# Windowed attention with a spatial gating block: spread of n, bias tables, weight conversion, size of the score groups, order

## The chip, the cores and the metric

The kernel runs on one core of a Trainium2 chip. What counts is the device time of one launch in microseconds (us). Before the change three runs took 471.61, 471.88 and 472.74 us, a median of 471.88 us. PE is TensorE with its matrix multiplications and PEld its weight loads; DVE is VectorE, ACT is ScalarE, POOL is GpSimd, and SP is SyncE, whose queue issues all DMAs here.

## What is computed

Attention over 4 batches, 8 heads and 768 tokens of 64 numbers; each token sees the first `n_global` (8) tokens and the last `n_local` (96), with a bias that falls with distance. Its output goes through a block that mixes the tokens of half of its features with a 768 x 768 matrix and multiplies the result with the other half.

```python
scores = scale * np.matmul(q, k.transpose(0, 1, 3, 2))
rel = pos[:, None] - pos[None, :]
is_global = pos[None, :] < int(n_global)
is_local = (rel >= 0) & (rel < int(n_local))
keep = is_global | is_local
dist = np.where(is_global & ~is_local, float(n_local), np.abs(rel))
scores = np.where(keep, scores + -slopes[:, None, None] * dist, -1e9)
a = softmax(scores)                       # along the keys
x = (a @ v)                               # heads side by side: 768 x 512 a batch
h = np.maximum(x @ w_in, 0.0)
u, v = h[..., :512], h[..., 512:]
v_n = (v - mean(v)) / np.sqrt(var(v) + 1e-06)
v_s = np.einsum('ts,bsd->btd', w_spatial, v_n) + b_spatial[None, :, None]
return (u * v_s) @ w_out
```

`w_in` and `w_out` come in as 64-bit floats, the rest as 32-bit floats, `n_global` and `n_local` as 64-bit integers.

## The kernel before

**Blocks.** The 768 tokens of a batch are 6 blocks of 128, so there are 24 blocks, numbered n over all batches. A block has scores against itself and, but for the first block of a batch, the block before it; the few global keys are copied into the ring of keys (`kring`).

**Steps of a block.** `scores(n)` (L1167) multiplies q and k for the 8 heads. Heads go in pairs, one on each 64-row half of PE; a pair is a matmul for either half, written side by side as one recorded operation (`halves64`, L122). VectorE takes the scores of a head from a PSUM bank, adds the bias table and finds the smallest entry (here called an eviction; `pr<-bank,bias` in the trace, followed by the reading of its result into `mn`), ScalarE takes the exponential (`pr<-pr,mn`), GpSimd or VectorE divides by the sum (`pr<-pr,rc`). `values(n)` (L1238) transposes the eight results on PE (`bank<-ident,pr`), copies them (`pth`), multiplies by v (`ops<-pth,vring`), and splits the result into a high and a low half (`xth`, `xtl`). The later matmuls use such halves, three products for one.

**The first six blocks** use whole 32-bit floats for q and k, one product for a pair. From block 6 on it is three products of halves. `size` (L1193) is the number of pairs in a group of scores: 4 in the first block of a batch, whose scores are 128 wide, else `SG`, which is 2. From block 6 on, a group of 2 is 12 matmuls and one of 4 is 24. A group is never broken by other work of PE, and holds a PSUM bank for every two pairs and half of rows where scores are 256 wide: two banks for a group of 2, four for a group of 4.

**Gating block.** `mlp_v`, `mlp_u`, `mlp_s` and `mlp_o` (L1277 to L1354; V, U, G and O in the schedule) are the four matrix products of the second part. They read `w_in`, `w_t` (the spatial matrix) and `w_out`, each as a high and a low half.

**Front.** Before that the kernel must load and build: the two numbers n (`nraw`, `nf`, `nwide`), the bias tables from them (`setup_bias`, L990: `bias0` for the first block of a batch, `bias` for the others, eight heads each), and the halves of the weights. `split_weights` (L1055) turns a tile of 128 x 512 64-bit floats into 32-bit halves: 8 tiles of `w_in`, 4 of `w_out`. It takes the sign apart, scales and clamps the upper word, shifts it into place and puts the sign on (the shift-and-or), masks the exponent out (the mask), multiplies the lower word by it (the product), and adds up. The tiles are `u`, `gh`, `gl` (as loaded), `raw`, `rawh` and `ev` in SBUF, and a PSUM bank.

**What sets the order.** All of this is first recorded, not issued. `plan` (L383) then sets every operation's place on its engine. It goes through time with a cost for every operation (`cost`, L243), a list of ranks (`RANKS`, L574: the lowest ready rank goes first) and pins (`PINS`, L827: the engine for an operation that could run on several), and it hands out six PSUM banks; two more hold `ops`. So a change in the number of operations needs new lists. Where the plan has a gap of more than 0.9 us on PE between 3.8 and 150 us, `keep_warm` (L544) fills it with transposes of the identity, `bank<-ident` in the trace. Nearly all instructions have the lines L47 or L49 in the trace, where they are issued.

Of the kernel before, what the change touches and what calls it, by code (L numbers as in the profile page):

```python
# [242 lines left out]
def cost(op):  # L243
# [6 lines left out]
    if op.eng == "tensor":  # L250
        if op.call == "transpose":
            return 109, 0, False
        if op.call == "halves64":
            n = elements(op.args[0]["rhs"])
            if op.args[0]["rhs"].dtype == F32:
                return 50 + len(op.args) * max(109, n * (.844 if list(op.args[0]["rhs"].ap)[0][1] < P else .422)), 0, False
            return len(op.args) // 2 * max(107, n * .461), 0, False
        n = elements(op.kw["rhs"])
        if op.kw["rhs"].dtype == F32:
            return max(234, 4 * n * .422), 0, False  # L260
        return {128: 111, 256: 120, 384: 177, 512: 232}[n], 0, False
    if op.eng == "sync":
        if n * parts <= 512:
            return 450, 600, False
        run = n // list(out.ap)[-1][1] * parts
        return (450 if run <= P and parts == P else 600 if run <= 256 else 1250), 120 + n * 4 * parts * .00243, False
# [27 lines left out]
    return (190 if parts < P else 74) + 1.04 * n + (0 if one else 60), 0, not one  # L294
# [249 lines left out]
def keep_warm(order, make):  # L544
# [996 lines left out]
```

## Time and profile before

| | us |
|---|---|
| median of 3 runs | 471.88 |
| the profiled execution | 472.18 |
| its span, first to last instruction | 470.4 |
| PE busy | 457.1 |
| VectorE busy | 313.3 |
| ScalarE busy | 202.6 |
| GpSimd busy | 180.6 |

The profiled execution's own time is 1.8 us longer than its span, and 0.3 us above the median. Busy time is a union of an engine's instructions; identity transposes count as busy on PE. In the trace a bank, a ring or a work tile has its name without its number. In a timeline, equal neighbours are drawn together with a count; matmuls overlap, so the pace of a run is the time from its start to the next start. An `issue` in the chain of waits is time in which an engine waited for nothing that the profile shows.

### The profile page before, as it was taken

How to read it: one execution, taken by the hardware profiler on the slowest of the kernel's cores; microseconds unless marked ns; L12 is line 12 of the kernel's file. 1: busy time of each engine (PE TensorE's matmuls, PEld its weight loads, DVE VectorE, ACT ScalarE, POOL GpSimd, SP SyncE). 2: the span in 40 equal slices, each digit the busy share in tenths (PEclk: the TensorE clock that was granted, in tenths of full speed). 3: DMA queues.
4: the chain of work that ended last, by engine and by line, in shares of the span. 5: the costliest groups of instructions: out<-in, count | busy, mean ns of one | idle time of the engine just before them, and what ended most of it. 6: DMA issues, size and time to landing. Idle time of an engine off the chain costs nothing.

```text
span 470.4 us, 9937 instructions
## 1 busy us (share of the span) xinstructions
PE 457.1 (97%) x3734; PEld 404.8 (86%) x3734; DVE 313.3 (67%) x947; ACT 202.6 (43%) x582; POOL 180.6 (38%) x285
## 2 busy tenths in 40 slices
PE   8888899999999999999999999999999999999996
PEld 8666679899888889889998889989998888989995
DVE  5999899973587678673338598985404688842343
ACT  2988665310364566652004675652113187320001
POOL 3788754451146656420115354351003163420021
PEclk9999899999999999999999999999999999999999
DMA  6947322410222323220012034220101211000012
GB/s 233 340 156 240 108 74 90 139 49 24 67 55 75 123 75 80 84 76 1 1 45 88 33 118 140 52 91 1 29 0 47 72 48 51 7 1 1 22 46 75
DMA packets 17816, 35.98 MB, mean 76 GB/s; under 512 B 2400, under 2 KB 2656, under 8 KB 17760
## 3 DMA queue, kind: packets, MB, share of 16 engines
q1 hardware_dynamic: 17760, 35.27, 22.9%
q8 instruction: 31, 0.51, 0.5%
q14 instruction: 25, 0.20, 0.1%
HBM read 28.97 MB, written 6.29 MB: 75 GB/s over the span
## 4 chain that ended last, share of the span: by engine, by line
PE 85%; DVE 9%; ACT 2%; POOL 1%; issue 1%; DMA 1%; SPq 0%; DVEq 0%; ACTq 0%; POOLq 0%
PE bank L49 71%; PE ops L47 7%; PE bank L47 7%; DVE bank L49 2%; DVE ev L49 2%; DVE pr L49 2%; POOL pr L49 1%; DMA nraw<-in_n_local_dram 1%; ACT pr L49 1%; DVE bias L49 1%; DVE w_in_l L49 1%; DVE rawh L49 0%; DVE raw L49 0%; DVE xtl L49 0%; ACT w_in_h L49 0%
## 5 line engine op out<-in xcount | busy, mean ns | idle before, releaser
L49 ACT ACTIVATE pr<-pr,mn 128x256 f32<-128x256 f32 (+1 forms) x192 | 92.3, 482 | 37.8 <-DVE mn L49 33.5
L49 DVE CUSTOM_DVE_ANT_0 pr<-bank,bias 128x256 f32<-128x256 f32 (+1 forms) x192 | 69.5, 395 | 27.7 <-PE bank L47 15.2
L49 POOL TENSOR_SCALAR pr<-pr,rc 128x256 f32<-128x256 f32 (+1 forms) x118 | 60.5, 525 | 45.9 <-DVE rc L49 34.2
L49 PE MATMUL bank<-ident,pr 128*128 128x128 f32 x352 | 59.1, 279 | 4.2 <-POOL pr L49 3.5
L49 ACT ACTIVATE ev<-bank 128x512 f32<-128x512 f32 (+1 forms) x37 | 21.5, 581 | 79.6 <-PE bank L49 38.7
L49 ACT ACTIVATE pth<-bank 128x512 f32<-128x512 f32 (+1 forms) x62 | 33.5, 552 | 50.3 <-PE bank L49 38.9
L49 PEld LDWEIGHTS bank<-ident,pr 128*128 128x128 f32 x352 | 41.5, 141 | 15.4 <-POOL pr L49 7.4
L49 DVE TENSOR_TENSOR ev<-bank,b_bc 128x512 f32<-128x512 f32 x24 | 16.4, 688 | 49.1 <-PE bank L49 46.1
L47 PE MATMUL bank<-kring,q 64*128 64x256 f32 (+1 forms) x528 | 46.4, 310 | 0.5 <-POOL kring L49 0.3
L49 PE MATMUL bank<-w_t_l,vnh 128*128 128x256 f32 x288 | 45.6, 283 | 0.0
L49 PE MATMUL bank<-w_t_h,vnh 128*128 128x256 f32 x288 | 44.7, 284 | 0.0
L49 PE MATMUL bank<-w_t_h,vnl 128*128 128x256 f32 x288 | 44.7, 282 | 0.0
L47 PEld LDWEIGHTS bank<-kring,q 64*128 64x128 f32 x528 | 36.0, 188 | 9.3 <-issue 4.2
L47 PE MATMUL ops<-pth,vring 128*64 128x128 f32 x704 | 43.7, 276 | 0.0
L47 PEld LDWEIGHTS ops<-pth,vring 128*64 128x64 f32 x704 | 37.9, 137 | 4.9 <-issue 3.4
L49 PEld LDWEIGHTS bank<-w_t_l,vnh 128*128 128x128 f32 x288 | 39.3, 189 | 1.0
L49 PEld LDWEIGHTS bank<-w_t_h,vnh 128*128 128x128 f32 x288 | 38.8, 189 | 0.9
L49 PEld LDWEIGHTS bank<-w_t_h,vnl 128*128 128x128 f32 x288 | 38.8, 189 | 0.9 <-issue 0.2
L49 ACT ACTIVATION_READ_ACCUMULATOR pr<-pr,mn 128x1 f32 x192 | 36.3, 189 | 0.0
L49 PE MATMUL bank<-xth,w_in_h 128*128 128x256 f32 x192 | 34.5, 289 | 0.5 <-DVE mn L49 0.5
L49 PE MATMUL bank<-xth,w_in_l 128*128 128x256 f32 x192 | 33.9, 287 | 0.0
L49 PE MATMUL bank<-xtl,w_in_h 128*128 128x256 f32 x192 | 33.6, 287 | 0.0
(127 smaller groups left out, 859.8 us busy)
## 6 DMA issues: line engine op xcount, KB each, us to landing
vring<-in_v_dram SPq DMA_DIRECT2D x24, 256.0 KB, 2.8
out_dram<-ev SPq DMA_DIRECT2D x23, 256.0 KB, 2.0
u<-in_moe_w_in_dram SPq DMA_DIRECT2D x8, 512.0 KB, 5.5
raw<-in_q_dram SPq DMA_DIRECT2D x9, 256.0 KB, 2.8
rawh<-in_q_dram SPq DMA_DIRECT2D x9, 256.0 KB, 2.6
raw<-in_k_dram SPq DMA_DIRECT2D x9, 256.0 KB, 2.7
rawh<-in_k_dram SPq DMA_DIRECT2D x9, 256.0 KB, 2.7
kring<-in_k_dram SPq DMA_DIRECT2D x6, 256.0 KB, 5.2
```

The lines of the kernel that those rows point to most:

```text
L47: self.real.matmul(**{n: placed(x) for n, x in kw.items()})
L49: getattr(self.real, self.call)(*[placed(x) for x in self.args], **{n: placed(x) for n, x in self.kw.items()})
```

## The change

Five things change.

- The numbers n are loaded to one partition instead of 128, turned into floats there, and spread by a matmul against a row of ones; VectorE copies the result from PSUM.
- The bias tables are built from maxima and minima with a large number instead of products with masks, in fewer steps. The scaling of `bias0` may run on ScalarE or GpSimd too.
- In `split_weights` the clamp comes before the scaling, the scaled tile goes to a PSUM bank, and the later steps go back and forth so that the shift-and-or, the product and both additions read at least one operand from PSUM. The mask reads SBUF and writes PSUM. The signed zero and the clamp are each done by VectorE or GpSimd.
- From block 6 on, a group of scores has four pairs.
- Some costs of the planner, all ranks and all pins are new, so the order is new on every engine.

```diff
 CFG = {
-    "WS": 6, "SG": 2, "WG": 4, "kept": "p", ...
+    "WS": 6, "conv": "pp", "SG": 4, "SG0": 2, "WG": 4, "kept": "p", ...
@@ cost
-            return len(op.args) // 2 * max(107, n * .461), 0, False
+            return 87 + len(op.args) // 2 * max(107, n * .461), 0, False
...
+    if op.call == "tensor_scalar" and not one and isinstance(op.kw.get("scalar1"), bass.AP):
+        return 130 + .54 * n, 0, True
...
-    return (190 if parts < P else 74) + 1.04 * n + (0 if one else 60), 0, not one
+    return (190 if parts < P else 74) + 1.04 * n + (0 if one else 60), 0, not (one and ("accum_out" in op.kw or any(in_psum(x) for x in op.reads) or len(op.reads) < 2))
@@ RANKS
-    -660.98, -553.57, -397.00, -559.33, ...
...
@@ attn_then_spatial_gating_kernel
-    nraw = const.tile([P, 4], I32, name="nraw")
-    nc.sync.dma_start(out=nraw[:, 0:2], in_=n_global.bitcast(I32).partition_broadcast(P))
-    nc.sync.dma_start(out=nraw[:, 2:4], in_=n_local.bitcast(I32).partition_broadcast(P))
-    nf = const.tile([P, 4], F32, name="nf")
+    nraw = const.tile([1, 4], I32, name="nraw")
+    nc.sync.dma_start(out=nraw[:, 0:2], in_=n_global.bitcast(I32).partition_broadcast(1))
+    nc.sync.dma_start(out=nraw[:, 2:4], in_=n_local.bitcast(I32).partition_broadcast(1))
+    row = const.tile([1, P], F32, name="row")
+    nc.vector.memset(row, 1.0)
+    nf = const.tile([1, 4], F32, name="nf")
...
+    spread = ps_m.tile([P, 2], F32, name="spread", tag="cv")
+    nc.tensor.matmul(spread, lhsT=row, rhs=none, start=True, stop=True)
+    nc.vector.tensor_copy(out=nwide, in_=spread)
@@ setup_bias
-        ts(out=g, in0=col, scalar1=ng, scalar2=None, op0=ALU.is_lt)
-        ts(out=far, in0=g, scalar1=-BIG, scalar2=BIG, op0=ALU.mult, op1=ALU.add)
-        ts(out=far, in0=far, scalar1=nl, scalar2=None, op0=ALU.add)
-        ts(out=loc, in0=rel, scalar1=nl, scalar2=None, op0=ALU.is_lt)
-        stt(out=loc, in0=rel, scalar=0.0, in1=loc, op0=ALU.is_ge, op1=ALU.mult)
-        tt(out=d_b, in0=rel, in1=loc, op=ALU.mult)
-        ts(out=t, in0=loc, scalar1=-1.0, scalar2=1.0, op0=ALU.mult, op1=ALU.add)
-        tt(out=d_0, in0=far, in1=t, op=ALU.mult)
-        tt(out=d_0, in0=d_0, in1=d_b, op=ALU.add)
+        ts(out=relp, in0=rel, scalar1=0.0, scalar2=BIG, op0=ALU.is_lt, op1=ALU.mult)
+        tt(out=relp, in0=relp, in1=rel, op=ALU.max)
+        ts(out=relb, in0=rel, scalar1=float(P), scalar2=None, op0=ALU.add)
+        ts(out=out_b, in0=relp, scalar1=nl, scalar2=BIG, op0=ALU.is_ge, op1=ALU.mult)
+        ts(out=g, in0=col, scalar1=ng, scalar2=BIG, op0=ALU.is_ge, op1=ALU.mult)
+        tt(out=d_b, in0=relp, in1=out_b, op=ALU.max)
+        stt(out=d_0, in0=g, scalar=nl, in1=d_b, op0=ALU.add, op1=ALU.min)
         for h in range(H):
-            ts(out=bias0[:, h], in0=d_0, scalar1=-slopes[h] / scale, scalar2=None, op0=ALU.mult)
+            scaled(None, bias0[:, h], d_0, -slopes[h] / scale)
         def more():
-            stt(out=d_b, in0=t, scalar=BIG, in1=d_b, op0=ALU.mult, op1=ALU.add)
-            ts(out=rel, in0=rel, scalar1=float(P), scalar2=None, op0=ALU.add)
-            ts(out=loc, in0=rel, scalar1=nl, scalar2=None, op0=ALU.is_lt)
-            ts(out=t, in0=loc, scalar1=-BIG, scalar2=BIG, op0=ALU.mult, op1=ALU.add)
-            tt(out=d_a, in0=rel, in1=loc, op=ALU.mult)
-            tt(out=d_a, in0=d_a, in1=t, op=ALU.add)
-            nc.vector.tensor_copy(out=d_a[:, 0:NGMAX], in_=far[:, 0:NGMAX])
+            ts(out=out_a, in0=relb, scalar1=nl, scalar2=BIG, op0=ALU.is_ge, op1=ALU.mult)
+            tt(out=d_a, in0=relb, in1=out_a, op=ALU.max)
+            ts(out=d_a[:, 0:NGMAX], in0=g[:, 0:NGMAX], scalar1=nl, scalar2=None, op0=ALU.add)
@@ split_weights
-            (nc.scalar, "activation", (m, upper.bitcast(F32), AF.Copy), dict(scale=2.0 ** -112)),
...
-        nc.vector.scalar_tensor_tensor(out=ci, in0=m.bitcast(I32), scalar=3, in1=ai, op0=ALU.logical_shift_left, op1=ALU.bitwise_or)
-        nc.vector.tensor_scalar(out=ai, in0=ci, scalar1=-0x800000, scalar2=None, op0=ALU.bitwise_and)
-        nc.vector.scalar_tensor_tensor(out=m, in0=lower.bitcast(U32), scalar=2.0 ** -52, in1=a, op0=ALU.mult, op1=ALU.mult)
-        cp(E("whi"), hi, c)
-        nc.vector.tensor_tensor(out=c, in0=c, in1=hi.bitcast(F32), op=ALU.subtract)
-        nc.vector.tensor_tensor(out=lo, in0=c, in1=m, op=ALU.add)
+        clamp = dict(out=m, in0=up, scalar1=UPPER_MAX, scalar2=-UPPER_MAX, op0=ALU.min, op1=ALU.max)
...
+            (nc.scalar, "activation", (c, m, AF.Copy), dict(scale=2.0 ** -112)),
...
+        stt(out=ai, in0=ci, scalar=3, in1=ai, op0=ALU.logical_shift_left, op1=ALU.bitwise_or)
+        ts(out=ci, in0=ai, scalar1=-0x800000, scalar2=None, op0=ALU.bitwise_and)
+        if CFG["conv"][x % len(CFG["conv"])] == "p":
+            stt(out=c, in0=lower.bitcast(U32), scalar=2.0 ** -52, in1=c, op0=ALU.mult, op1=ALU.mult)
+            tt(out=c, in0=c, in1=a, op=ALU.add)
+            cp(E("whi"), hi, c)
+            tt(out=lo, in0=c, in1=hi.bitcast(F32), op=ALU.subtract)
+            return
@@ scores
-        size = NP if i == 0 else CFG["SG"]
+        size = NP if i == 0 else CFG["SG0"] if whole_s(n) else CFG["SG"]
```

Here `c` is the tile in PSUM, `a` and `m` are tiles in SBUF.

What the new order is, at three places. First VectorE at the tables, about its first eviction; `ev` tiles hold distances, an `ISA` with a bank as operand is an eviction, one with `mn` alone reads its result. Before:

```order
L49 TENSOR_SCALAR bias_94<-ev_106 128x128
L49 TENSOR_SCALAR bias<-ev_106 128x128 [waits DVE_49]
L49 TENSOR_SCALAR bias<-ev_106 128x128
L49 ISA pr_115,mn_107<-bank_87,bias_94 128x128 [waits DVE_49,PE_49]
L49 ISA mn_107 128x1
L49 TENSOR_SCALAR bias_94<-ev_106 128x128 x3
L49 ISA pr_109,mn_107<-bank_87,bias_94 128x128 [waits DVE_49]
```

After, from the copy of n to the first eviction:

```order
L49 COPY nwide<-bank_89 128x2 [waits PE_49]
L49 TENSOR_SCALAR ev_107<-ev_106,nwide 128x128 [waits DVE_49,Pool_49]
L49 TENSOR_SCALAR ev_107<-ev_106,nwide 128x128
L49 TENSOR_SCALAR wide<-nwide 128x1
L49 TENSOR_SCALAR ev_107<-ev_106,nwide 128x128
L49 TENSOR_TENSOR ev_108<-ev_106,ev_107 128x128 [waits DVE_49] x2
L49 TENSOR_SCALAR ev_108<-ev_107,nwide 128x32 [waits DVE_49]
L49 TENSOR_SCALAR bias<-ev_108 128x128 [waits DVE_49]
L49 TENSOR_SCALAR bias<-ev_108 128x128
L49 SCALAR_TENSOR_TENSOR ev_108<-ev_107,nwide,ev_108 128x128
L49 TENSOR_SCALAR bias<-ev_108 128x256 [waits DVE_49]
L49 TENSOR_SCALAR bias<-ev_108 128x128 x3
```

Behind this come one more 128x1 step and the first eviction, which waits for PE and ScalarE. The scaling for the first block (`bias_94`, now `bias_96`) has left VectorE, and all table work stands ahead of the evictions.

Second PE's start. Before, 33 identity transposes and the scores of block 0 stand first; then, with the last scores of a group of block 1 ahead:

```order
L47 MATMUL bank_89<-kring_103,q_0_102 128x256
L47 MATMUL bank_90<-kring_103,q_0_102 128x256
L49 MATMUL bank_92<-ident 128x128 x71
L49 MATMUL bank_92<-ident,pr_109 128x128
L49 MATMUL bank_92<-ident,pr_110 128x128
L47 MATMUL bank_88<-kring_103,q_0_102 128x256
```

After:

```order
L49 MATMUL bank_89<-ident 128x128 x33
L49 MATMUL bank_89<-none,row 128x2
L49 MATMUL bank_90<-ident 128x128 x34
L47 MATMUL bank_90<-kring_105,q_0_103 128x128
L47 MATMUL bank_91<-kring_105,q_0_103 128x128
```

The scores of block 0 now stand behind the spread of n (`none,row`) and 34 more identity transposes, and 11 transposes follow them in place of 71. In SP's queue the loads of block 0's k and q, first behind n before, now stand behind those of another q, v and a tile of `w_in`; k is the fourth load behind n, a second tile of `w_in` the fifth and q the sixth.

Third PE at a later block of the first kind, the end of a group of scores. Before, 12 matmuls on two banks, then the products with v and those of the gating block; the block's other group of 12 comes 24 rows later:

```order
L47 MATMUL bank_88<-kring_153,q_0_151 128x256
L47 MATMUL bank_90<-kring_153,q_0_151 128x256
L47 MATMUL ops_100<-pth_125,vring_117 64x128 x2
L47 MATMUL ops_100<-pth_126,vring_117 64x128 x2
L47 MATMUL ops_100<-pth_131,vring_117 64x128 x2
L47 MATMUL ops_100<-pth_132,vring_117 64x128 x2
L49 MATMUL bank_87<-w_out_h,gh_160 128x512 x2
```

After, the middle of a group of 24:

```order
L47 MATMUL bank_93<-kring_155,q_0_154 128x256
L47 MATMUL bank_89<-kring_155,q_0_154 128x256
L47 MATMUL bank_90<-kring_155,q_0_154 128x256
L47 MATMUL bank_91<-kring_155,q_0_154 128x256
```

The second pair of banks follows the first with nothing between. In the whole order before, 21 runs of scores have 12 matmuls and 8 have 24 (one of the 21 is block 0 with a half of block 1); after, 18 runs have 24 and none 12.

## Rows read from the trace of the kernel before

**Rows 1.** The page, busy time, share of the span and instructions of each engine.

```profile
PE 457.1 (97%) x3734; PEld 404.8 (86%) x3734; DVE 313.3 (67%) x947; ACT 202.6 (43%) x582; POOL 180.6 (38%) x285
```

**Rows 2.** Table by stage: busy us of each engine (instructions), granted clock, DMA share, GB/s.

```profile
12.00:24.00 12.00, 9.74 (x76) 7.62 (x75) 10.98 (x54) 11.67 (x40) 8.98 (x20) 1.00 0.91 340
24.00:48.00 24.00, 21.23 (x164) 15.79 (x164) 22.81 (x64) 20.24 (x57) 20.38 (x27) 1.00 0.55 186
48.00:60.00 12.00, 10.65 (x70) 7.32 (x66) 10.28 (x32) 7.64 (x22) 8.86 (x17) 0.86 0.42 125
60.00:84.00 24.00, 23.29 (x203) 20.09 (x200) 23.60 (x61) 14.06 (x36) 12.27 (x20) 1.00 0.22 73
84.00:465.90 381.90, 381.90 (x3156) 344.29 (x3154) 239.16 (x705) 145.42 (x422) 126.19 (x194) 1.00 0.17 55
```

**Rows 3.** Timeline of PE, start: start us, length us, instruction, operands, count.

```profile
1.71 5.58 PE L49 MATMUL bank<-ident 128*128 128x128 f32 x33 [1.71 <-POOL ident masks.py:199]
...
9.42 7.97 PE L49 MATMUL bank<-ident 128*128 128x128 f32 x71
```

**Rows 4.** Chain of waits from 7.2 to 72.7 us, its shares by engine and name.

```profile
by line: DVE bank L49 15.3%; DVE ev L49 12.2%; DVE pr L49 11.7%; issue 10.3%; POOL pr L49 7.6%; ACT pr L49 5.0%; PE bank L49 4.5%; DVE bias L49 4.0%; DVE w_in_l L49 3.8%; DVE rawh L49 3.4%; PE bank L47 3.1%; DVE raw L49 2.4%; DVE xtl L49 1.
```

**Rows 5.** Timeline of VectorE, from 8 to 15 us.

```profile
8.28 0.28 DVE L49 TENSOR_TENSOR ev<-ev 128x128 f32<-128x128 f32 x1
8.48 0.28 DVE L49 TENSOR_TENSOR ev<-ev,ev 128x128 f32<-128x128 f32 x1
...
9.71 0.28 DVE L49 CUSTOM_DVE_ANT_0 pr<-bank,bias 128x128 f32<-128x128 f32 x1
...
9.92 2.17 DVE L49 TENSOR_SCALAR bias<-ev 128x128 bf16<-128x128 f32 x3
...
12.66 0.22 DVE L49 TENSOR_SCALAR ev<-ev 128x128 f32<-128x128 f32 x1
...
14.25 0.43 DVE L49 TENSOR_SCALAR bias<-ev 128x128 bf16<-128x128 f32 x2
```

**Rows 6.** ScalarE by shape to 24 us: count, busy us, mean ns, idle before.

```profile
L49 ACT ACTIVATE bias<-ev 128x256 bf16<-128x256 f32 x3 | 1.1, 401 | 0.0
L49 ACT ACTIVATE bias<-ev 128x128 bf16<-128x128 f32 x4 | 0.9, 292 | 0.0
```

**Rows 7.** DMA over the first 12 us: GB/s in 40 slices of 0.3 us.

```profile
GB/s 0 0 0 0 0 0 1 1 1 1 0 0 0 103 41 55 76 123 362 403 416 389 416 410 389 434 423 420 393 399 451 417 423 382 434 420 399 451 468 396
```

**Rows 8.** VectorE by shape from 7.2 to 84 us: count, busy us, mean ns, idle before.

```profile
L49 DVE SCALAR_TENSOR_TENSOR bank<-ev,raw 128x512 int32<-128x512 int32 x5 | 6.0, 1196 | 0.6 <-POOL ev L49 0.4 <-ACT pth L49 0.2
...
L49 DVE SCALAR_TENSOR_TENSOR ev<-u,rawh 128x512 f32<-128x512 uint32 x4 | 3.4, 851 | 0.0
L49 DVE SCALAR_TENSOR_TENSOR bank<-ev,rawh 128x512 int32<-128x512 int32 x4 | 3.4, 841 | 0.1
L49 DVE SCALAR_TENSOR_TENSOR ev<-u,raw 128x512 f32<-128x512 uint32 x4 | 3.1, 770 | 0.0
```

**Rows 9.** Instructions of VectorE on PSUM banks to 84 us: shortest, median, longest ns.

```profile
L49 DVE TENSOR_TENSOR w_in_l<-bank,ev x8: 676/680/691, 21.6 to 73.2; 128x512 fp32r<-128x512 f32 x8
...
L49 DVE TENSOR_SCALAR raw<-bank x5: 659/691/694, 16.7 to 77.2; 128x512 int32<-128x512 int32 x5
```

**Rows 10.** Timeline of GpSimd and VectorE around 47 us.

```profile
46.34 1.84 POOL L49 TENSOR_TENSOR w_t_l<-gh,w_t_h 128x768 fp32r<-128x768 f32 x1
...
46.85 1.88 DVE L49 SCALAR_TENSOR_TENSOR bank<-ev,raw 128x512 int32<-128x512 int32 x1
```

**Rows 11.** Timeline of PE around a group of 12 and one of 24 scores.

```profile
127.03 0.98 PE L47 MATMUL bank<-kring,q 64*128 64x256 f32 x12
127.93 0.39 PE L49 MATMUL bank<-w_t_l,vnh 128*128 128x256 f32 x1
...
153.11 1.69 PE L47 MATMUL bank<-kring,q 64*128 64x256 f32 x24
154.73 0.44 PE L49 MATMUL bank<-ident,pr 128*128 128x128 f32 x2
```

More of the change, by code (lines that the diff above doesn't have):

```diff
@@ L260, in cost @@
             return max(234, 4 * n * .422), 0, False
-        return {128: 111, 256: 120, 384: 177, 512: 232}[n], 0, False
+        return {128: 111, 256: 120, 384: 177, 512: 233.5}[n], 0, False
     if op.eng == "sync":
@@ L264, in cost @@
             return 450, 600, False
-        run = n // list(out.ap)[-1][1] * parts
-        return (450 if run <= P and parts == P else 600 if run <= 256 else 1250), 120 + n * 4 * parts * .00243, False
+        return 450, 120 + n * 4 * parts * .00243, False
     if op.eng == "scalar":
@@ L868 @@
-    "---"
+    "---------------------------202----------------000------------0-----20-100011111-00-------110-------1"
+    "1--------0-0--------01----------0--0-----------00-------1---------------0-1-----0--------00-------10"
+    "0----0---0--------21--------------0-------------0----------0-0-------------0000--------------------0"
+    "0--21--1-----------0-------------00--------------------------001--------------------20--------------"
+    "-------------------------------------21-20------0----0------------0------0---------------------0----"
@@ new lines @@
+    "------------------2---------0--000------------0----0-----------0110----0--------------------1--0----"
+    "---------------21---------------------------------------------------001----0--111-------2--11-------"
+    "--1------------0010---------0-------------1011-------------------20---------------------------------"
+    "---------------------------------------1-11--0--------------00-0--0----0-----------0010-------------"
+    "--------------------------111---------------------------------------1------------------------------1"
@@ new lines @@
+    "-0-----0-----------------1-1-----------1-------------111--------------------------------------------"
+    "-------------------------------------1-----------------------------20-11---------1-----------011----"
+    "-0----1--------------1011---------------------------------------100---------------------------------"
+    "----1-1----------------------------------------------01---------------------------------------------"
+    "--------------------------01-10----------------------111----0------1------------0--0----------------"
@@ new lines @@
+    "-----1-0--11---------------------11-0----1----0-1------------101------------------------------------"
+    "-------------------------------------1--1----------1------------01-------------1-------------1------"
+    "---------------0------------------20----------------------------------------------------0-01--1-----"
+    "---------101---0--1-1-----------1000---------------------------------------1-1----------------------"
+    "---------------1-------------------------------1--2-----0------------------------1------1-----------"
@@ new lines @@
+    "-011------------------------------------------1-------------------------------------10--------------"
+    "-----------------0-2------------------------01----1----1-1-------------0-1--------------------------"
+    "-------------021--------------------------------------01--------------------------------------------"
+    "--0--------------------0---------------------------------------------------20-01----0----0----------"
+    "---------0--------------------0-0---------------------0-10--0----0----1-----------0-1-----1---------"
@@ new lines @@
+    "----------010--------------------11------------------------------------------------------10----1----"
+    "0------------0001----1----1-------------0000-------------------20-------------------1---------------"
+    "------------------------------------01-21--0--------------0101-----0-------------100----------------"
+    "------------------------01---------------------------------------10--------------------------------0"
+    "1----0----0-------------0----------0-0---------------0---------------------------------------001----"
@@ new lines @@
+    "---------------------------------121------------------------------0--1----1----0-----------1-10----0"
+    "----1-0--------------01---------------------------------------111-----------------------------------"
+    "---2-----------------------------------------------2-------------------21---------------------------"
+    "------------------------11-11----1----------------0-0----------0-1------------000-------------------"
+    "---1-01-11----0----------------00------0----1--------------1010-------------------10----------------"
@@ new lines @@
+    "--------------------------------------1----0---------1-1---------------------------------------20---"
+    "------------------------------------------------------------------------------------001-------------"
+    "------------------------021-----------------------------------------------------------------120-----"
+    "--------------------------------1-------------------------------------------------------------------"
+    "-11----------------------------------------------------------------------------------"
@@ L995, in setup_bias @@
         d0 = work.tile([P, 4, P], F32, name="d0", tag="ev", bufs=nb("ev"))
-        rel, col = place[:, 0], place[:, 1]
+        rel, col, relp, relb = (place[:, x] for x in range(4))
         nc.gpsimd.iota(rel, [[-1, P]], base=0, channel_multiplier=1, allow_small_or_imprecise_dtypes=True)
@@ L1069, in split_weights @@
         ci, ai = c.bitcast(I32), a.bitcast(I32)
-        sign = dict(out=a, in0=upper.bitcast(F32), scalar1=0.0, scalar2=1.0, op0=ALU.mult, op1=ALU.mult)
+        ts, stt, tt = nc.vector.tensor_scalar, nc.vector.scalar_tensor_tensor, nc.vector.tensor_tensor
+        up = upper.bitcast(F32)
+        sign = dict(out=a, in0=up, scalar1=0.0, scalar2=1.0, op0=ALU.mult, op1=ALU.mult)
         any_of((nc.vector, "tensor_scalar", (), sign), (nc.gpsimd, "tensor_scalar", (), sign))
+        clamp = dict(out=m, in0=up, scalar1=UPPER_MAX, scalar2=-UPPER_MAX, op0=ALU.min, op1=ALU.max)
@@ L1072, in split_weights @@
+        any_of((nc.vector, "tensor_scalar", (), clamp), (nc.gpsimd, "tensor_scalar", (), clamp))
         any_of(
-            (nc.scalar, "activation", (m, upper.bitcast(F32), AF.Copy), dict(scale=2.0 ** -112)),
-            (nc.vector, "tensor_scalar", (), dict(out=m, in0=upper.bitcast(F32), scalar1=2.0 ** -112, scalar2=None, op0=ALU.mult)),
-        )
-        clamp = dict(out=m, in0=m, scalar1=UPPER_MAX * 2.0 ** -112, scalar2=-UPPER_MAX * 2.0 ** -112, op0=ALU.min, op1=ALU.max)
-        any_of((nc.vector, "tensor_scalar", (), clamp), (nc.gpsimd, "tensor_scalar", (), clamp))
@@ new lines, in split_weights @@
+            (nc.vector, "tensor_scalar", (), dict(out=c, in0=m, scalar1=2.0 ** -112, scalar2=None, op0=ALU.mult)),
+        )
+        stt(out=ai, in0=ci, scalar=3, in1=ai, op0=ALU.logical_shift_left, op1=ALU.bitwise_or)
[6 more added lines that the diff above has]
+            return
@@ L1085, in setup_w_in @@
+        stt(out=m, in0=lower.bitcast(U32), scalar=2.0 ** -52, in1=c, op0=ALU.mult, op1=ALU.mult)
+        two(None, m, m, a, ALU.add)
+        cp(None, hi, m)
+        two(None, lo, m, hi.bitcast(F32), ALU.subtract)
     def setup_w_in(b, half):
```

47 lines of the change are left out of this document (4 added, 43 removed), and 503 rows, old and new, of tables (CFG, RANKS).

## Prediction

> **What bounds the kernel now.** I read the page first: TensorE (PE) is busy for 97% of the span, VectorE for 67% [rows 1]. The table by stage shows what that average hides. From 84 to 465.9 us PE has no idle time at all, and VectorE works for 239 of 382 us. From 24 to 84 us VectorE is busy for 22.81 + 10.28 + 23.60 = 56.7 of 60 us, and PE has holes [rows 2]. So there are two regimes: a front in which VectorE and what it feeds (ScalarE's exponentials, GpSimd's normalisation) lead and PE waits, and a long rest in which only PE's own work counts.
>
> What PE loses in the front bounds what a better front can give. Idle from 12 us on: 2.26 + 2.77 + 1.35 + 0.71 = 7.1 us [rows 2]. To this come the identity transposes that only keep PE awake: after the first 33 the program holds 71 + 7 + 11 = 89, at the 7.97 / 71 = 0.112 us of the long run 10.0 us [rows 3]. And from 48 to 60 us the granted clock was 0.86 in the mean, so for a part of it at the lower of the two levels (1.2 instead of 2.4 GHz), beside 1.35 us of idle PE; 0.14 x 12 = 1.7 us [rows 2]. Together 19 us. The chain of waits from 7.2 to 72.7 us is led by VectorE: the names of VectorE that its row still shows make up 53%, all its pieces together 39.7 of 65.5 us, a share of 0.61 [rows 4]; the rest is handovers, ScalarE, GpSimd and a little PE.
>
> **The change, part by part.**
>
> *Spread of n and the tables.* Before, the two numbers land on 128 partitions and VectorE works on them at once. Now they land on one, and a matmul against a row of ones spreads them. They may land earlier, but that buys nothing: the spreading matmul stands in PE's queue behind the 33 identity transposes, which end at 1.71 + 5.58 = 7.29 us [rows 3]. With the matmul and the copy back (no row; bounds 0.2 and 0.6 us, one and three dependent steps of VectorE at 0.2 us from start to start [rows 5]; I take 0.4) n is there at 7.7 us. From there ten VectorE instructions lead to the table of block 0, at 0.2 us each: 9.7 us. ScalarE and GpSimd scale it, ScalarE behind tables of 128x128 and three times 128x256, 0.29 + 3 x 0.40 us [rows 6] from about 9.2 us: 10.7 us. PE has 34 more identity transposes ahead of the first scores, 34 x 0.112 = 3.8 us, so scores start at 11.2 us and the first eviction at about 11.7 us, where it was at 9.71 us [rows 5]: **2.0 us lost**. Tables and scaling hide behind PE with about a microsecond to spare, and so do the loads: six of them, the last the first q (four of 256 and two of 512 KB, 2.05 MB), now stand before the scores, and at the 0.4 MB per us seen from 5.4 us on [rows 7] they have landed by about 10.1 us. If that cover is gone, the first eviction slips by as much.
>
> What comes back: after its first eviction VectorE before still builds tables, three scalings that end at 12.01 us (2.09 us), then eight small steps of 0.14 + 0.47 + 0.55 us, the first at 12.66, the last two from 14.25 us [rows 5], 3.25 us in all. Now one 128x1 step is left there. **Net: -1.25 us of VectorE's time.**
>
> *Conversion of the weights.* Twelve tiles of 512 columns, with five long VectorE instructions each before and after. What differs is how many operands lie in SBUF. Up to 84 us the shift-and-or from two SBUF tiles into PSUM took 1196 and 841 ns in the mean (nine of them, 9.4 us), the product of the lower words 851 and 770 ns (eight, 6.5 us) [rows 8]. An addition that reads one operand from PSUM took 676 to 691 ns in all eight cases, the mask from PSUM 659 to 694 [rows 9]. One case shows the reason: GpSimd's subtraction of two SBUF tiles ran from 46.34 to 48.18 us, and VectorE's shift-and-or, begun at 46.85, took 1.88 us and ended 0.55 us behind it [rows 10]. The excess over 0.68 us is 9.4 - 9 x 0.68 = 3.3 us and 6.5 - 8 x 0.68 = 1.1 us. In the new order both read one operand from PSUM: **-4.4 us**. One thing no row shows: the mask now reads one SBUF tile and writes PSUM. Its nearest rows are the mask before, never held, and the shift-and-or, held by 0.37 us in the mean; over the eight masks of the front that is 3.0 us back. Nothing below zero, as no 512-column step that touches PSUM was shorter than 0.66 us. I take zero, by the first row: the same operation, one operand on either side. 3.0 us stays as the other end.
>
> The Trainium skill speaks to this in SBUF — State Buffer, section Who interferes with whom: a VectorE instruction with at most one SBUF input, outside its two-port modes, does not contend with GpSimd; one with two SBUF inputs contends with a GpSimd instruction that reads SBUF. By that rule the mask costs nothing; by the shift-and-or's row this part would shrink to 1.4 us. The trace agrees on the half about two inputs (1.88 us beside GpSimd's 1.84); no run here yet shows the other half with the result in PSUM.
>
> VectorE's time in the front falls by 1.25 + 4.4 = 5.65 us. I let only its share of the chain reach PE, since ScalarE and GpSimd stand behind it and get no faster: 5.65 x 0.61 = **-3.4 us**. Bounds: 0 (another engine leads) and -5.65 us. That signed zero, clamp and scaling change places among GpSimd, ScalarE and VectorE I cost at nothing, under the cover of the same chain; without it each swap is a step of 0.4 to 0.8 us. The 89 identity transposes become 34 + 11 + 8 + 12 = 65, 24 x 0.112 = 2.7 us of PE: no term of its own, but of the size of 3.4.
>
> *Four pairs a group.* A group of 12 score matmuls takes 127.93 - 127.03 = 0.90 us, one of 24 takes 154.73 - 153.11 = 1.62 us [rows 11], so a second group costs PE 0.18 us. In the later part 10 blocks have their two groups apart before, 5 adjacent; now all 15 are in one. This lies where PE never waits: 10 x 0.18 = **-1.8 us**. The price is four of six PSUM banks at once; the eight groups of 24 that stand there before pay no PE stall for it [rows 2].
>
> *New order.* The other matmuls are the same, the last 366 of the program too; I take no change at the end.
>
> **Sum.** The profiled execution took 472.18 us (span 470.4, 1.8 around it), 0.3 above the median of 471.88. 472.18 - 3.4 - 1.8 = 467.0 us.
>
> **The rivals.**
>
> *The front gives nothing.* ScalarE is busy 11.67 of 12 us from 12 to 24 us and 20.24 of 24 after that [rows 2], and it gets four more 128x128 and two more 128x256 tables, 4 x 0.29 + 2 x 0.40 = 2.0 us, ahead of the first exponentials. If ScalarE eats VectorE's lead, only the groups are left: 472.18 - 1.8 = 470.4 us. Against it: from 48 us on a third of ScalarE's time is free.
>
> *The mask is held after all*, and the new operands don't do what they are for: 3.0 x 0.61 = 1.8 us back, 468.8 us.
>
> *More than forecast.* VectorE's whole 5.65 us reach PE and the slow clock (1.7 us) goes too: 472.18 - 5.65 - 1.7 - 1.8 = 463.0 us. For it: 19 us of PE's loss are there. Against it: a fifth of the chain's named time is GpSimd's and ScalarE's [rows 4].
>
> *PE stalls at the large groups* (the other side). While a block's eight evictions run, two banks are left for everything else. One eviction takes about 0.35 us from start to start, so two of the four banks come back after 1.4 us. If half of that is lost at each of the ten new places, it is 7 us: 467.0 + 7 = 474.0 us. From 0.52 us a place on it outweighs the gain. For it: few banks. Against it: no idle PE beside the groups of 24 that exist.
>
> **How the numbers follow.** Forecast 0.49 (464.8 to 469 us); front gives nothing 0.18; mask held 0.08; more 0.15; stalls 0.10. A measurement of this kernel tells about 0.3% (1.4 us) from no change. Faster by more than that: 0.49 + 0.08 + 0.15 and half of 0.18 (470.4 lies on the edge), 0.81; within it, the other half and a little of the stalls, 0.11; slower 0.08. The range takes in the front that gives nothing and the near side of "more", and leaves out the stalls and the far side: 462.9 to 471.2 us.
>
> **What would show it.** Right: first eviction near 11.7 us; shift-and-or, product and mask of 512 columns all near 0.68 us; fifteen groups of 24 at 1.62 us; PE without idle from some 80 us on; idle plus identity transposes of the front down from 17 to about 14 us. Wrong: a mask as long as the GpSimd instruction beside it, ScalarE without holes from 12 to 40 us, or PE idle behind a group of 24.

## The result, and the profile after

The changed kernel takes 465.82 us (median of 4 runs, 465.49 to 466.25), the kernel before 471.75 us beside it (470.31 to 472.74). The ratio is 0.9877 (95% interval 0.985 to 0.9905): 5.9 us less. The profiled execution has a span of 463.8 us, 6.6 us less than before. The forecast was 467.0 us, 5.2 us less than the profiled execution before (472.18 us); the profiled execution after took 465.66 us.

First the engines' row of the page, which answers to [rows 1], then the table by stage, which answers to [rows 2] (busy us of each engine and its instructions, granted clock, share and GB/s of the DMA engines).

```profile
PE 449.2 (97%) x3712; PEld 402.2 (87%) x3712; DVE 299.8 (65%) x922; ACT 205.1 (44%) x593; POOL 194.3 (42%) x295
```

```profile
12.00:24.00 12.00, 6.80 (x49) 4.84 (x45) 10.88 (x42) 9.70 (x35) 10.98 (x18) 0.80 0.78 289
24.00:48.00 24.00, 21.23 (x160) 15.94 (x156) 22.54 (x68) 18.64 (x54) 18.46 (x28) 0.96 0.72 236
48.00:60.00 12.00, 11.68 (x116) 9.33 (x116) 11.65 (x42) 10.74 (x30) 7.76 (x15) 1.00 0.11 33
60.00:84.00 24.00, 24.00 (x218) 21.92 (x217) 21.73 (x61) 14.83 (x38) 12.03 (x20) 1.00 0.30 92
84.00:459.30 375.30, 374.96 (x3106) 340.20 (x3104) 227.92 (x682) 146.51 (x425) 141.56 (x201) 1.00 0.17 55
```

VectorE works 299.8 us in place of 313.3, PE 449.2 in place of 457.1. PE is without idle time from 60 us on but for one wait of 0.34 us at 168 us, and nearly so from 48 us; before, it had lost 1.35 us from 48 to 60 us and 0.71 us after that. But the start is worse than it was: from 12 to 24 us PE works 6.80 us (9.74 before), and the granted clock is 0.80 there and 0.96 in the next stage, where it was 1.00. So the gain has not come at the beginning. PE's timeline shows what happens there (start, length, instruction, operands, count, idle time before it and what ended it):

```profile
7.35 0.38 PE L49 MATMUL bank<-none,row 1*128 1x2 f32 x2
...
11.52 1.16 PE L47 MATMUL bank<-kring,q 64*128 64x128 f32 x16
...
13.96 1.13 PE L47 MATMUL bank<-kring,q 64*128 64x256 f32 x8
20.25 2.34 PE L49 MATMUL bank<-ident,pr 128*128 128x128 f32 x8 [5.15 <-POOL pr L49]
22.52 2.08 PE L47 MATMUL bank<-kring,q 64*128 64x256 f32 x8
24.54 1.84 PE L47 MATMUL ops<-pth,vring 128*64 128x128 f32 x16
...
33.80 0.44 PE L49 MATMUL bank<-ident,pr 128*128 128x128 f32 x2 [1.57 <-DVE pr L49]
...
48.32 1.14 PE L47 MATMUL bank<-kring,q 64*128 64x256 f32 x8 [0.72 <-DVE mn L49]
```

The hole of 5.15 us is new. Before, 71 identity transposes stood behind the first scores [rows 3]; now 34 stand ahead of them and 11 behind. The program fills a gap only with a PSUM bank that is free through all of it, and here conversions and scores leave it none. By slices of 4 us:

```profile
16.00:20.00 4.00, 0.00 (x0) 0.00 (x0) 4.00 (x14) 3.64 (x13) 3.76 (x9) 0.91 1.04 384
20.00:24.00 4.00, 3.70 (x16) 2.48 (x16) 3.71 (x11) 2.28 (x8) 3.49 (x5) 0.50 0.26 91
24.00:28.00 4.00, 4.00 (x34) 2.89 (x31) 2.54 (x13) 2.92 (x10) 3.29 (x5) 0.74 0.88 277
```

Behind the hole the clock is at 1.2 GHz, half of full speed (0.50 from 20 to 24 us). Eight score matmuls then take 2.08 us, where the same eight take 1.13 us at 13.96.

VectorE at the start, answering to [rows 5]:

```profile
2.74 0.22 DVE L49 SCALAR_TENSOR_TENSOR none<-none,nf 1x1 f32<-1x1 f32 x2
7.77 0.16 DVE L49 COPY nwide<-bank 128x2 f32<-128x2 f32 x1 [4.81 <-PE bank L49]
...
12.83 0.29 DVE L49 CUSTOM_DVE_ANT_0 pr<-bank,bias 128x128 f32<-128x128 f32 x1 [1.46 <-PE bank L47]
```

The two numbers are ready at 2.96 us, then VectorE waits 4.8 us for the spread, which stands in PE's queue behind 33 transposes. No table work is left behind the first eviction. That eviction begins at 12.83 us; the forecast had 11.7.

The conversion up to 84 us, by shape (count, busy us, mean ns), answering to [rows 8] and [rows 9]:

```profile
L49 DVE SCALAR_TENSOR_TENSOR bank<-u,bank 128x512 f32<-128x512 uint32 x8 | 5.5, 689 | 0.0
...
L49 DVE SCALAR_TENSOR_TENSOR raw<-bank,raw 128x512 int32<-128x512 int32 x6 | 4.1, 683 | 0.0
...
L49 DVE TENSOR_SCALAR bank<-raw 128x512 int32<-128x512 int32 x5 | 3.4, 687 | 0.0
...
L49 DVE TENSOR_SCALAR bank<-rawh 128x512 int32<-128x512 int32 x4 | 2.7, 679 | 0.0
```

Shift-and-or, product and mask of 512 columns: all between 679 and 689 ns in the mean.

### The profile page after: what moved, and what is told of

Same layout as the page of the kernel before. It is cut to its first block, busy times and chain, and to the rows that moved or that the text cites. A ratio compares the mean times of both kernels' runs of the same rounds, so it can differ in the third digit from the quotient of the medians.

```text
span 463.8 us, 9906 instructions
## 1 busy us (share of the span) xinstructions
PE 449.2 (97%) x3712; PEld 402.2 (87%) x3712; DVE 299.8 (65%) x922; ACT 205.1 (44%) x593; POOL 194.3 (42%) x295
## 4 chain that ended last, share of the span: by engine, by line
PE 90%; DVE 4%; DMA 3%; issue 1%; SPq 0%; POOL 0%; ACT 0%; DVEq 0%
PE bank L49 73%; PE ops L47 8%; PE bank L47 8%; DMA u<-in_moe_w_in_dram 2%; DVE pr L49 1%; DMA vring<-in_v_dram 1%; DVE bank L49 1%; DVE w_in_l L49 1%; SPq L49 0%; POOL pr L49 0%; DVE rawh L49 0%; DVE xtl L49 0%; DVE q L49 0%; DVE rc L49 0%; DVE ev L49 0%
## 5 line engine op out<-in xcount | busy, mean ns | idle before, releaser
L49 POOL TENSOR_SCALAR pr<-pr,rc 128x256 f32<-128x256 f32 (+1 forms) x115 | 55.5, 495 | 53.6 <-DVE rc L49 26.1
L49 PE MATMUL bank<-ident,pr 128*128 128x128 f32 x352 | 54.3, 279 | 7.6 <-POOL pr L49 5.9
L49 ACT ACTIVATE pth<-bank 128x512 f32<-128x512 f32 (+1 forms) x67 | 36.2, 560 | 37.2 <-PE bank L49 33.7
L47 PE MATMUL bank<-kring,q 64*128 64x256 f32 (+1 forms) x528 | 43.6, 307 | 0.7 <-DVE mn L49 0.7
L49 PE MATMUL bank<-w_t_l,vnh 128*128 128x256 f32 x288 | 44.2, 282 | 0.0
L49 PE MATMUL bank<-w_t_h,vnh 128*128 128x256 f32 x288 | 42.9, 282 | 0.0
L49 PE MATMUL bank<-w_t_h,vnl 128*128 128x256 f32 x288 | 42.8, 282 | 0.0
L47 PEld LDWEIGHTS bank<-kring,q 64*128 64x128 f32 x528 | 35.0, 188 | 8.2 <-issue 3.7
L49 POOL TENSOR_TENSOR gl<-ev,gh 128x512 fp32r<-128x512 f32 x14 | 18.1, 1293 | 53.3 <-PE bank L49 34.7
L49 DVE TENSOR_SCALAR pr<-pr,rc 128x256 f32<-128x256 f32 (+1 forms) x77 | 32.2, 443 | 0.5
```

The costliest lines, as they stand in the source:

```text
L47: self.real.matmul(**{n: placed(x) for n, x in kw.items()})
L49: getattr(self.real, self.call)(*[placed(x) for x in self.args], **{n: placed(x) for n, x in self.kw.items()})
```

## The experiments

All stand against an unaltered copy of the changed kernel, the control. The runs "operands back in SBUF", "groups cut in two" and "hole filled" were taken beside it, on one chip. "Both undone", the first try of "spread earlier", "fewer of the old transposes" and "the start moved up" ran on a second chip, where the kernel before took 471.96 us (471.95 beside the control); the others ran later on the first chip (471.56 us). The edits are given in words, not as code.

**The control.** 

> The changed kernel, unaltered, as the mark that the other three stand against on the same chip. All theories: about 465.8 us, ratio to the kernel before near 0.988, first eviction at 12.8 us, PE without idle time from about 49 us on.

Measured: 466.23 us (465.1 to 466.66), ratio to before 0.9876 (0.9847 to 0.9905).

**The operands back in SBUF.** After the planning, so that order and engines stay:

```diff
-scaled upper word: c (PSUM);   ai = c << 3 | ai;   ci = ai & exponent
-c = lower * 2**-52 * c;        c = c + a
+scaled upper word: m2 (SBUF);  ci = m2 << 3 | ai;  ai = ci & exponent
+m2 = lower * 2**-52 * a;       c = c + m2
```

> The changed kernel with the operands of the weight conversion back where they were: the scaled upper word lies in SBUF (a tile of its own), the shift-and-or reads two SBUF tiles and writes PSUM, the mask goes from PSUM to SBUF, the product of the lower words is from SBUF to SBUF. The same instructions on the same engines in the same order, nothing else. Theory (VectorE's 4.4 us of contention were worth their share of the chain, 0.61): shift-and-or near 1.0 to 1.2 us and product near 0.85 us instead of 0.68, and 2.7 us more than the control; 4.4 us if all of it reaches TensorE. Rival (the new order won the front, and VectorE has slack for long operands): the same longer instructions, but less than 1 us more than the control.

Measured: 468.18 us (467.43 to 468.95), 1.95 us above the control, and no run of the one lies among those of the other. VectorE by shape up to 84 us:

```profile
L49 DVE SCALAR_TENSOR_TENSOR conv<-u,raw 128x512 f32<-128x512 uint32 x4 | 4.3, 1069 | 0.0
L49 DVE SCALAR_TENSOR_TENSOR bank<-conv,raw 128x512 int32<-128x512 int32 x5 | 4.0, 807 | 0.0
...
L49 DVE SCALAR_TENSOR_TENSOR bank<-conv,rawh 128x512 int32<-128x512 int32 x4 | 3.5, 878 | 0.0
...
L49 DVE SCALAR_TENSOR_TENSOR conv<-u,rawh 128x512 f32<-128x512 uint32 x4 | 3.3, 830 | 0.0
```

The long forms are back: 4.0 + 3.5 us for nine shift-and-ors and 4.3 + 3.3 us for eight products, 15.1 us, where 17 x 0.68 would be 11.6. Set against these 3.5 us of VectorE's time, the 1.95 us at the end are a share of 0.56. But GpSimd, which stands on the other side of the contention, is also longer: 200.6 us in the whole page where the changed kernel has 194.3; of these 6.3 us more, 5.1 lie up to 84 us. One normalisation, begun at 38.97 us beside a product and a shift-and-or of VectorE, takes 1.41 us, where 0.48 is usual. Which of the two engines carries how much of the 1.95 us was not taken apart. The rival (slack) falls.

**The groups cut in two.**

```diff
+for each group of 24 matmuls of 256 columns (10 of 15):
+    issue 12; issue the next matmul or transpose of PE's queue; issue the other 12
```

> The changed kernel with ten of its fifteen groups of 24 score matmuls of 256 columns cut in two groups of 12, the next matmul or transpose of TensorE's queue between the halves, as many as stood apart before. Theory (a second group costs TensorE 0.18 us, rows of the trace before, and TensorE never waits there): 1.8 us more than the control, TensorE still without idle time from 49 us on. Rival 1 (the gain of the rest came from elsewhere in the new order): within 0.5 us of the control. Rival 2 (four banks at once hurt the changed kernel): faster than the control.

Measured: 469.81 us (469.05 to 470.45), 3.58 us above the control: twice the forecast, with PE as free of idle time as before. PE's timeline shows why. First the changed kernel, one group of 24; then the same place cut, and a second place that is cut by a transpose.

```profile
134.86 1.69 PE L47 MATMUL bank<-kring,q 64*128 64x256 f32 x24
136.48 1.20 PE L49 MATMUL bank<-w_in_h,xth 128*128 128x512 f32 x4
```

```profile
134.53 0.98 PE L47 MATMUL bank<-kring,q 64*128 64x256 f32 x12
135.44 0.50 PE L49 MATMUL bank<-w_in_h,xth 128*128 128x512 f32 x1
135.87 0.97 PE L47 MATMUL bank<-kring,q 64*128 64x256 f32 x12
136.76 0.97 PE L49 MATMUL bank<-w_in_h,xth 128*128 128x512 f32 x3
...
143.03 0.98 PE L47 MATMUL bank<-kring,q 64*128 64x256 f32 x12
143.94 0.33 PE L49 MATMUL bank<-ident,pr 128*128 128x128 f32 x1
144.19 0.98 PE L47 MATMUL bank<-kring,q 64*128 64x256 f32 x12
145.10 0.55 PE L49 MATMUL bank<-ident,pr 128*128 128x128 f32 x3
```

The uncut group goes from 134.86 to 136.48, 1.62 us. Cut, it goes from 134.53 to 136.76, 2.23 us; less the 0.23 us that one 512-column matmul takes in a row of its kind (0.92 us for four, from 44.73 to 45.65 us of the changed kernel), 2.00 us, so 0.38 us more. Each half ends with the 0.18 us that I had read from [rows 11]. But the matmul between the halves also takes 135.87 - 135.44 = 0.43 us to the start of the next instead of 0.23: going *into* a group costs as well, and that time stands in the row of the instruction ahead, which I had not looked at. The transpose takes 0.25 instead of 0.11 us: 143.03 to 145.10 is 2.07, less 0.11, less 1.62 is 0.34 us. Six of the ten places are cut by a transpose, four by another matmul; in the mean 0.36 us a place, ten times 3.6 us. PE itself says the same: from its first cut group to its last matmul it takes 327.82 us (134.53 to 462.35), where the changed kernel takes 324.27 (134.86 to 459.13): a difference of 3.55 us.

**Both undone.** The two edits above in one kernel.

> The changed kernel with the conversion's operands back in SBUF and, together with that, ten of the fifteen groups of 24 cut in two: what is left of the change is the spread of n, the earlier tables, the swapped engines of sign and clamp, and the new order. The two alone cost 1.95 us (468.18 against 466.23) and 3.58 us (469.81 against 466.23). Theory (they lie in different stages and add up, and the rest of the change is worth nothing): 466.2 + 1.95 + 3.6 = 471.8 us, within 0.7 us of the kernel before. Rival (the rest of the change carries a gain of its own of a microsecond or more, or the two share a path): below 470.8 us.

Measured: 471.54 us (470.73 to 472.55), ratio to before 0.9998 (0.9984 to 1.0013). Operands and groups carry the whole gain and add up (1.95 + 3.58 = 5.5 us, both together 5.3 above the control); the spread of n, the tables, the swapped engines and the new order are together worth nothing that can be measured. That is a net: it holds the loss in the hole, where PE waits 6.76 us and the clock is 0.78 from 12 to 24 us in this run too, and so a gain elsewhere that makes up for it.

**The spread earlier.**

```diff
-33 identity transposes; spread of n; 34 identity transposes; scores
+12 identity transposes; spread of n; 21 + 34 identity transposes; scores
```

> The changed kernel with the matmul that spreads n moved ahead of 21 of the 33 identity transposes that stand before it: the two numbers are ready at 2.96 us in its trace, and VectorE then waits 4.8 us for the spread. Theory (the first scores stand behind all the transposes in TensorE's queue, so earlier tables buy nothing there): VectorE's tables begin at about 4.3 instead of 8.0 us, first eviction unmoved near 12.8 us, time within 0.5 us of the control's 466.2. Rival (ScalarE and GpSimd, free of the tables 3.5 us earlier, convert earlier, and that is on the chain): 1 to 2 us less.

This one took 2235.8 us: the 21 transposes wrote over the spread numbers before they were copied out, so that the program computed everything twice, the second time by its general path; its time says nothing here. With another target for the transposes:

> The spread of n moved ahead of 21 of the first 33 identity transposes, once more; these 21 now write a stretch of PSUM that nobody uses, since in the first try they wrote over the two spread numbers before VectorE had copied them, and the program took its branch for long ranges. Expectations as for the first try: theory (the first scores stand behind all the transposes in TensorE's queue) VectorE's tables from about 4.3 us instead of 8.0, first eviction unmoved near 12.8 us, within 0.5 us of the control's 466.2; rival (ScalarE and GpSimd convert earlier, and that is on the chain) 1 to 2 us less.

Measured: 466.01 us (465.68 to 466.81), ratio to before 0.988 (0.9861 to 0.9898), the same as the changed kernel. VectorE has the numbers at 5.08 us and then waits for the scores all the same:

```profile
5.08 0.16 DVE L49 COPY nwide<-bank 128x2 f32<-128x2 f32 x1 [1.93 <-PE bank L49]
...
12.96 0.29 DVE L49 CUSTOM_DVE_ANT_0 pr<-bank,bias 128x128 f32<-128x128 f32 x1 [5.02 <-PE bank L47]
```

**The hole filled.**

```diff
 scores of the second block (first half)
+44 identity transposes into PSUM that is free until 36 us
 transposes of the first block's probabilities
```

> The changed kernel with 44 identity transposes more, behind the scores that end at 15.1 us, in the hole of 5.15 us ahead of the transposes of 20.25 us; they write a stretch of PSUM that nobody uses until 36 us. Theory (the granted clock, 0.50 from 20 to 24 us and 0.74 from 24 to 28 us, has TensorE on the chain at half its pace there): granted clock 1.00 through 12 to 28 us, and 1.5 to 3 us less than the control. Rival (VectorE and GpSimd lead there, TensorE only waits longer for the probabilities): full clock, but within 0.5 us of the control.

Measured: 461.83 us (461.78 to 462.3), ratio 0.9788 (0.976 to 0.9815), 4.4 us less than the control; built and run once more, on the same chip, 462.08 us, as below. By stage and on PE's timeline:

```profile
12.00:24.00 12.00, 11.55 (x104) 9.75 (x105) 10.73 (x43) 9.89 (x36) 11.52 (x20) 1.00 0.77 281
24.00:48.00 24.00, 23.27 (x197) 17.62 (x192) 23.89 (x85) 21.26 (x64) 20.93 (x34) 1.00 0.72 239
```

```profile
20.70 0.66 PE L49 MATMUL bank<-ident,pr 128*128 128x128 f32 x4 [0.20 <-POOL pr L49]
21.61 0.78 PE L49 MATMUL bank<-ident,pr 128*128 128x128 f32 x4 [0.25 <-ACT pth L49]
22.31 1.33 PE L47 MATMUL bank<-kring,q 64*128 64x256 f32 x8
23.57 1.09 PE L47 MATMUL ops<-pth,vring 128*64 128x128 f32 x16
...
30.13 1.09 PE L49 MATMUL bank<-ident,pr 128*128 128x128 f32 x8
...
44.68 1.20 PE L47 MATMUL bank<-kring,q 64*128 64x256 f32 x8
```

The clock stays at 1.00. The transposes come no earlier (20.70 us; this execution's first 33 transposes ended 0.45 us later), but the eight, the scores and the values behind them end at 24.59 instead of 26.31 us: 2.2 us with the later start counted. The rest comes downstream: the changed kernel waits 1.57 us at 33.80 and 0.72 us at 48.32 for VectorE, and here neither wait is left; the scores of 48.32 start at 44.68. TensorE at half its pace was on the path, and the rival falls.

**Fewer of the old transposes.** The hole filled, the last 20 of the old ones taken out.

> The kernel with the hole filled (461.8 us), without the last 20 identity transposes that the program held before (8 at 25.7 us and 12 at 31.3 us in its trace). Theory (TensorE leads its chain from 31.3 us on, the 12 stand on that chain, the 8 don't): 12 x 0.112 = 1.3 us less, about 460.5 us, with the clock at 1.00 throughout. Rival (the clock falls again in the gaps that they filled): granted clock below 1 between 24 and 40 us, and 461.8 us or more.

Measured: 462.59 us (462.25 to 463.01), no gain, and both theories are wrong: the clock stays at 1.00, but PE waits in their place.

```profile
32.77 1.14 PE L47 MATMUL bank<-kring,q 64*128 64x256 f32 x8 [1.39 <-POOL kring L49]
```

Of the 20, the 12 that begin at 31.27 us with the hole filled stood on the chain as it is drawn; the chain only showed that PE was busy, not that the instruction behind them could have begun earlier. GpSimd's copy of the global keys sets that start.

**The start moved up.** The hole is filled here too.

```diff
-first loads: q of a late block, v, w_in, k, w_in, q, ...
+first loads: k, q, w_in, k, q, w_in, w_sp, ...
-33 transposes; spread of n; 34 transposes; scores
+ 8 transposes; spread of n; 20 transposes; scores
```

> The kernel with the hole filled (461.8 us), and the start moved up: 25 of the first 33 and 14 of the next 34 identity transposes are left out, and the first loads after the two numbers are the first block of k, of q and of w_in; the load of a q block that is used much later goes behind the others. Theory (the start up to the first scores lies on the chain): first eviction at about 8 us instead of 13, and 2 to 4 us less, 458 to 460 us. Rival 1 (the loads of w_in and w_sp, at 0.4 MB per us from 2 to 17 us, set the pace of the conversions whatever the scores do): first eviction as early, but within 0.7 us of 461.8. Rival 2 (TensorE has longer holes then, and the clock falls): granted clock below 1 between 10 and 24 us, and more than 461.8 us.

Measured: 463.98 us (462.54 to 464.81), about 2 us *more* than with the hole filled alone (on the other chip), although the first eviction begins at 8.96 us. PE, then an instruction of ScalarE that stands ahead of the copies `pth`:

```profile
18.54 0.66 PE L49 MATMUL bank<-ident,pr 128*128 128x128 f32 x4 [2.36 <-POOL pr L49]
...
21.19 2.08 PE L47 MATMUL bank<-kring,q 64*128 64x256 f32 x8
```

```profile
19.02 0.84 ACT L49 ACTIVATE w_t_h<-gl 128x768 fp32r<-128x768 f32 x1 [2.11 <-DMA gl<-in_moe_w_spatial_dram]
```

The hole is 2.36 us longer than the transposes in it and ends with GpSimd's normalisations; the granted clock is 0.86 from 12 to 24 us, and eight scores take 2.08 us again. That is rival 2. Beside it ScalarE stands 2.11 us before a load of `w_sp`, until 19.02 us, with the copies `pth` queued behind it that PE's next transposes wait for (0.99 us, at 20.19): a load holds the front, as rival 1 says, though its number (within 0.7 us) is missed. How the 2 us divide between the two isn't shown. So both were mended:

> The kernel with 44 identity transposes in the hole of 15.1 to 20.25 us, once more, as the mark for the next run on the same chip: 461.8 us, clock 1.00.

Measured: 462.08 us (461.61 to 462.87).

> The start moved up as in the last such run (which took 464.0 us, with a hole of 2.36 us and the granted clock at 0.86 from 12 to 24 us, and ScalarE waiting for a load of w_sp that landed at 19.0 us), with two things mended: 54 identity transposes in the hole instead of 44, and three loads that are not read before 55, 62 and 106 us (two q blocks and the bias row, 0.9 MB, at 0.4 MB per us some 2.2 us of the DMA engines) stand behind the first 20 others. Theory (clock and loads were what ate the earlier start): first eviction near 9 us, granted clock 1.00 from 12 to 24 us, transposes of the first block 2 us earlier than with the hole filled alone, and 1 to 2.5 us less than that, 459.3 to 460.8 us. Rival (ScalarE and GpSimd set the pace from 24 us on whatever the start does): within 0.7 us of 461.8 us.

Measured: 461.27 us (460.8 to 462.77), ratio 0.979 (0.9769 to 0.9811): the lowest median, but the runs overlap those of its mark, so a gain over it isn't shown. The clock is mended (1.00 in the first row, 12 to 24 us), so is the load (ScalarE begins on that tile at 17.13 us without a wait), and PE's transposes start at 18.83 instead of 20.70 us. GpSimd, at work without a wait from 12.34 us on, sets that start (second row: its eight normalisations). The 1.9 us have shrunk to 0.8 us by the scores of 43.92 (44.68 with the hole filled alone).

```profile
12.00:24.00 12.00, 10.25 (x93) 8.54 (x92) 11.65 (x42) 9.56 (x33) 11.56 (x17) 1.00 0.75 259
```

```profile
16.65 2.82 POOL L49 TENSOR_SCALAR pr<-pr,rc 128x128 f32<-128x128 f32 x8
```

```profile
18.83 0.66 PE L49 MATMUL bank<-ident,pr 128*128 128x128 f32 x4 [1.50 <-POOL pr L49]
...
43.92 1.20 PE L47 MATMUL bank<-kring,q 64*128 64x256 f32 x8
```

## Why the prediction came out as it did

| Step | Forecast, us | Measured, us | From |
|---|---|---|---|
| Operands in PSUM | 4.4 x 0.61 = 2.7 | 1.95 | operands back in SBUF |
| Spread and tables | 1.25 x 0.61 = 0.8 | not measured alone; none together with the swapped engines and the new order | both undone |
| Groups of four pairs | 1.8 | 3.6 | groups cut in two |
| Sum | 5.2 | 5.9 (median against median) | |

That the total was near is luck: the groups were priced 1.8 us too low, the front 1.5 us too high.

*The groups* were the step that failed most, by its size. "A second group costs PE 0.18 us" took the difference of two rows, and each row ends where the next begins, so it held only the way out of a group. With 0.36 us a place in place of 0.18 the term doubles. The way in stands in the row before. The mechanism (it lies where PE never waits, ten places) was right. The Trainium skill's TensorEngine Tiling (Array Packing), section Key Properties, says that a change of tiling mode drains TensorE. The trace agrees so far as both changes cost time: 0.36 us for in and out together.

*The operands.* The mechanism was right in every row: with one operand in PSUM nothing is held, with two in SBUF it is. Too high was the amount: the 4.4 us were those of the old order, in the new one the old operands cost 3.5 us. The share of 0.56 is near the 0.61 that I took, but one of its reasons failed: that ScalarE and GpSimd "get no faster". GpSimd does, by 6.3 us, and the share leaves that out. The mask was rightly put at zero: 679 and 687 ns. The Trainium skill's SBUF — State Buffer, section Who interferes with whom, says that a VectorE instruction with at most one SBUF input, outside the two-port modes, does not contend with GpSimd. The trace agrees, now also with the result in PSUM.

*The first eviction* was forecast for 11.7 us and came at 12.83. The scores started at 11.52 (forecast 11.2); I had let the eviction follow them by 0.5 us, but it waits for the whole first group, 16 matmuls and 1.16 us. It had no price that was shown: tables 2.7 us earlier change nothing, and an eviction 4 us earlier (8.96 us) gained nothing that was shown, with a load, GpSimd and the clock in its way. By these runs the 2.0 us on the side of the loss should have been near zero. The 3.25 us of table work that VectorE no longer has behind that eviction were not put back by themselves: what they are worth stays open.

*What I costed at nothing* was the hole. "The 89 identity transposes become 34 + 11 + 8 + 12 = 65" stood in the text as a saving of PE's time; I didn't ask which stretch they had kept awake, and of the 71 behind the first scores 11 were left. Idle time and identity transposes together were to fall from 17 to 14 us; they are 5.20 + 2.77 + 0.32 us idle and 65 x 0.112 = 7.3 us, 15.6 in all, and the slow clock costs, by the same estimate from its mean, 0.20 x 12 + 0.04 x 24 = 3.4 us, where it cost 1.7. I named the slow clock only as something that could go ("more than forecast"); it grew, and the kernel with the hole filled shows 4.4 us for it. What makes up for that loss, so that the rest of the change comes out at nothing, wasn't taken apart; candidates are the table work that is gone, the swapped engines, the order, and the slow stretch from 48 to 60 us, which is gone (1.00 in place of 0.86).

*The rivals.* ScalarE has 2.3 us of holes from 12 to 24 us: no bound. The mask isn't held. PE has no idle time at the groups of 24 (374.96 of 375.30 us from 84 us on; the 0.34 us are a wait for VectorE's `pth` at 168 us, not at a group). PE is free of idle time from 49 us instead of the 80 I named: the front does get shorter, behind the hole.

## What to carry to other kernels

Read the cost of a change of mode on both sides of the group: the instruction ahead of it carries half. Before transposes that only keep TensorE awake are dropped, or a planner drops them for want of a bank, ask what the clock does in the hole they leave: here 44 of them, 4.9 us of work that nobody reads, made the kernel 4.4 us faster than without them. And a chain of waits says what was busy last, not what could have started earlier: of three edits at the front (transposes out, tables earlier, first scores earlier) none gained anything that was shown.

## What the runs showed of the hardware that I had not expected

- A change between matmuls on half of the rows (64) and on all of them costs 0.14 to 0.20 us on the way in and 0.18 us on the way out, here 0.36 us a group.
- In a hole of 5.15 us TensorE's granted clock fell from 2.4 to 1.2 GHz (0.50 from 20 to 24 us, 0.74 from 24 to 28); scores take their usual 1.13 to 1.14 us again only from 26.31 us on, 6 us into the work that followed. With that one hole filled the kernel took 4.4 us less of 466.
- The contention is felt on both sides: with two SBUF operands on VectorE, GpSimd's busy time rises by 6.3 us as well (194.3 to 200.6).
